# A fused attention and gated long convolution: turning the softmax weights of three batches by DMA instead of by TensorE, and cutting the last inverse transform by positions

## The chip, the core and the metric

The kernel runs on one core of a Trainium2 chip. A core has TensorE (PE, the matrix products; the loading of a product's stationary operand is shown apart as PEld), VectorE (DVE), ScalarE (ACT) and GpSimd (POOL). A further engine, SP, issues transfers, and so do POOL and ACT. The metric is the device time of one execution in microseconds (us), the median of several runs. A profile is one execution recorded by the hardware profiler. Its span runs from the first to the last instruction.

## What is computed

There are two chained attentions and then a gated convolution:

```
p_packed = softmax(scale * p @ k^T) @ v          # 32 packed queries per head
x        = softmax(scale * q @ p_packed^T) @ p_packed   # 576 positions, 8 heads of 64
proj     = x @ w_proj                            # 512 -> 3*512
x1, x2, x3 = proj split in three
x2_conv  = irfft(rfft(x2) * rfft(filter), n=576) # along the positions
out      = (x1 * x2_conv * x3) @ w_out
```

There are 8 batches. q, k and v have 8 heads, 576 positions and 64 features. The model width is 512.

## The kernel before

**The stages.** Each batch passes through four generator functions. `front` (lines 706 to 870) turns k and q, forms the first attention, and leaves the second attention's softmax weights: `a2`, 128 positions in the partitions by 4 tiles x 256 columns (8 heads x 32 packed keys), and a fifth tile of 128 columns with the last 64 positions, both halves of the keys side by side. The weights are normalised by one POOL product over 1152 columns (`a2n<-e,zr`, line 843; on DVE for batch 0). `turn` (872 to 932) multiplies the packed values into w_proj (`qm`, 892), takes the forward transform of the weights by products with constant tables (`fp`, `fpt`, 899 to 919; `ez` on ACT, then `fa` on POOL) and **turns the weights** so that the packed keys lie in the partitions: ten TensorE transposes of 128 columns per batch (`a2tp`, 923 to 929), five into each of two PSUM tiles, and one DVE copy of 576 columns per tile into `a2t` (930). `middle` (934 to 986) forms the spectrum (`f`, five pieces of 128 frequencies, 943), multiplies it by the filter on DVE (`tt`, 953) and combines it on POOL: two sums of 1024 columns (957) and four `gm` pieces of 512 (962); the fifth piece of `gm` comes from DVE. Beside it, `gate` (964) forms x1 and x3 as products of `qm` with `a2t`, 512 columns of positions at a time for each of four blocks of features, and a rest of 64. Per block x1 goes through an ACT copy (`x1s`) and a DVE product into `w`. `back` (989 to 1069) forms the inverse transform (`inverse`, 1018: `x2`, three products over the 288 even positions with `gm` 0, 1, 4 and three over the 224 odd ones with `gm` 2, 3, 4 per block of features), multiplies by `w` on DVE (`y`, 1030) and projects by w_out (`project_out`, 1033: `o`, five groups of positions, split in two halves of 256 columns in the last batch), from where ACT or DVE scale into `os` (5 buffers) and a transfer writes the result.

**The order.** All instructions are recorded first (`Recorder`, 221). `PRIORITY` (86) is a compressed list with one number for each instruction. It shifts the instruction's place in the recorded order. `plan` (306) gives these to `schedule` (316), which walks through the instructions with an estimate of each one's duration (`Op.ns`, 166; transfers in `transfer_ns`, 193) and takes, on each engine, the ready one with the lowest number. The order that comes out is then fixed for each engine (`emit`, 534). So the whole order, on all engines, hangs on the list: there is no loop order that survives it. All profiled instructions carry line 538, the line that emits them; they are told apart by the names of their tiles. In PE's gaps up to 34 us by the planner's clock, `spin` products (1112) that compute nothing are put in.

**Queues.** POOL issues all loads, which cast fp32 to fp16. SP issues the result's writes and, for batches 4 to 7, transposing DMAs: q turned into `qT` (one per batch, 16 blocks of 128x128), and for batches 6 and 7 the keys into `kT` (four per batch, 6 blocks of 96 rows each). SP works in order: a transfer that waits holds up those behind it.

Of the kernel before, what the change touches and what calls it, by code (L numbers as in the profile page):

```python
# [14 lines left out]
FP16 = mybir.dt.float16  # L15
AF = mybir.ActivationFunctionType
ALU = mybir.AluOpType
AX = mybir.AxisListType

P = 128  # L20
# [23 lines left out]
def _constants(S):  # L44
# [42 lines left out]
    'c-oy-2|QHm`#)ziBV@}q$-b}ILqe1#S<_+(QCblyS-Q3q6)7nx*OIa&WG5L#Qp%bw`;vWM;+D?&kC{0$!@d8{?{|OiG0r*f`<(aLzR&l0g<vs='  # L87
    '-skz=M^>B>C98^O79=;F+~z2#*^_&Aw(_gw@3h6d`$6M;p%eO@bfY=Fi=#RWN-2G@iNBm%a|9kab)~&68y;M>&-z&J>u@98+tu6WNM5tTp1|z#'
    'qN=p|rB#7u465h(xW9?n6X6(xO9%Y5o!Y~Vd5uTyvI9)Kk{_km+>Y2kq&E`(wW?P9sFRkdd!Sr^NE}AYes9%X?nBnbHmZ_nD-Bnas&><q?Gdd@'
    'agRzO9Fs4eI)1LutKQ+6yGz~G@Al~}em{~bQltED8=tkdw>WMUq+8?k^4OId=CA0)CUW!yJMK1h$A^2>XrHn<=si!HtR58dY7^%lTfApvBP(j}'  # L90
    'XK1H#MvGZi2Wh<=RN*mR3Ti#4ZRBGnWvrmze8J~}flqdhj1?a@tLLPO-KJTUX{YU%gA*f#YdP}n^tMYCwvDSg>leK~BH%1@WQaM_M%9T=PUB?X'
    'ZNCl=5AztGcz<EZH~dD8o>?L)TmO8V=kd$l)U2K-cHqeS4zwuGiM{S%C~vW(*VE9)(9JM5h3cXi-|Ml8<t)%=&!Q&>r6rE$u|9?z?(KcA{=p~2'
    'WY1y1W@QGqS;LH%|A&_L@z9f27oDSnnVpXDT~s#H_ElnbK5OM;d_j%<x*Ux?!yaX<l%j~Xw~?UKG`lX1oVp>~sxnV%xfQ#R=d%9MR9i00`{vFF'
    'lpvS1%pvy|ZPIRs9tYU%E!=j4u@Y;8jj!GJu-D}JPFv1=FRlrbmRaA218rDgjc`9%u+l2~1WPLK$-}SA1w4=V3tmv86_XyGw_n=6IwG#lHl)uc'
    'HO;MFtrvo808<2A_z&q%Vqe}^Rw@r>URiBD9C5CdcUW~-{554`eJ_*#DD!Wjz0m?~P{|CtUsvI-r(*UdahGo&4e2_;&BnBNStAatUoCUDoaE3?'
    'YDO<-)ckh*8vlDx;+)sPKm2ACs>QxzSOSHXxii&(FNRY!$)I%sdM*oVj`m265bg3{%S!G!@6~T$F&A6!`nvC3t1{1=k{?s2q7jFq>c0K9tzSFp'
    'a;AMHx?Kzfop-tJwDdLdm*6?6z$L^jZ+1d=hnb)0aeXzc-Whj)b_ruMN!`<W7p#wK$;nr0sVi}SUh!|EP7K;^MPHRQ)DFTLS=_xDqNv6(+cMsp'
    '08}ybEYk|{*$Bxn6ktS8@6%c3?3&`brYGg#>=k-2Le6%}t<<Q74-RVKAJ00)+WILgSEhSq+J}0FCwWAL-8*&5x@!L0W5(mUhwlV4J`r)2ZVa!%'
    ';(A1~2Esn+XDKJkq8TDJm_&*muvzU~)Irr4<Vx2HCXJSX#h+suRHkbF<P3X1UO!Z(Q{G*Rdb(6m)1KF{qNNq3e@5T$_ioeQbK4GYI$3Z6Ug>1#'
    '%#Ij$Po1h;3ZyxLxhf$b#QyA7<;`7RO}&e6mseJQoG3D#%zeh8a(*wLoVv=2x-h?~+X+2-Md|HIEYb?9iu^pg#94LpC2V%esbZJ4nYH$a@`~)_'  # L100
    '4tw*`o9zf+#Oe5nkHbr%g+_73+vsc?<TMSO1NVI5f5OTr|4~)>y<Z2%F?7EDDyPIN!(YsaQOceM=&`d(Sdm|hBJ7fX<<QP;OMLFtv7lq_cyCEi'
    'R-)ohVGHe7{g*}TI&{bH4@Eodr=fRYm6(s8$eL_lO2;|&UhH-0I-VEsywW2}HT=}djDkl9t*th{i2QGPld6Ly^qjRu(_@b^uEl6BajQ!4H<as%'
    'E{MjqT1>cz38x64#<VTpK7E~#_eXl!8&!<YL}TKZY<CJawAH6f%$dPp(SkQ)I;ME;fJ<Q1)pT6Z$mJEObA8`3%jZvo_}_oqnp*tjTxMCv$|Hdg'
    'lS0o^F6k~ISTie~u3(v+d`zmn<z;gXEkECmRgZnCrb+5-eewO<yBEE6_3yHq^P5sfvOab7eEwP)*I6=FTer~mSMj}6QF#H)@f$x*`FeC1F4b=x'
    '>M(ED3jd?kp3YuNyx&qx!tTKS)fP_I=IwKD_KRAp+IZQR7#JzA#JMd_?o4NmMTJUfObbYHpJ1z2qZguuB6}HSIRy(w>hr#>pa#Y)ZC>Y>%eU+f'
    '9Gr>#)HiU;Oih+;cu(;sZ@X)W?;@U`PCs4{Q~j=6RBH5?13w!Zzp`OGZ+Z9Ng$mD7W1L5@Wq`YvSFnX+LF=qM!>=7Y+a|Bw;+O9hKJb#QVrS%R'
    'acUde*N7KIv1Xp{s`wv#iOlR3K!>PADHaU<tm|D^$R0o|&^|WGIGh}meKl8;WzeZP>R{O2=Ald7I@aY41%ti8QggLU35?ssN8)^~3!Z?`ZadaX'
    'X`d4PT3%c`jnm3%sX+5=UKJ`k>t?Le!oM(ab5U40kA>aCh5ulua5c_7@wQuRwEMl={+Ay(2Ho-Uwfo~j?7cUJcWtjbI%_&#*74cD$NzAc+wFU1'
    ';l{yN4NymD`_-77r$4W*4%s}4?B5rK^LKb(9crN+_;V^>^U7Jrm^v=ruM4w`heV=^)7k@sVghpG-&)KZ{B$rbIk^G8LPM{|I|7)y(eB?X<6h-#'
    'ZrZs;*Tz%c!qX#8mgVf{=(wYA<i9)Azm6BIj=p<K_<2HR8msu7i?lL&30~*gbn;VC=iGnH+VDM9YoM<<G$@&~t4#fAcy_?U8@K&e>1Usf>QDaE'  # L110
    'Qi*is!<cS6irsb0H_SZ#v4H7Jt;Oc>olEDxT{E<f-aWEoyvg<uss}wh^j4eRO-tE0=sOGjwYxV1!Xg4M#iupp&9_%_wQm~ChZ2~al48=oEj{d*'
    '4y?`U&dI<fgyKHr)r8>^s*?um3!BsDlY+X_@4mV9BsJ~X%gBz37hzB7jGbB-yzb&UKBmW|NQ5}szdzX>)RWy*FW6V}>GgtT;_8)WuQDzs%XDmi'
    ')&05j`ZDv(Hfc^x-ATjCZi1{^VsTe;Ubg*ta)^aXceCawn^Ov#Xq#Ko3!I+cxffgA^}^ymsAI)hCYYA`mZy7P756q^goa}y+yZZS1EK;l82Gh<'
    'Z|$$CG`WMS1{3#cidB7YWO^TE9uE`XY1`)%rg3q<$`zM@ikO@OU2b{V+;aW%!;4GIM+=L&gsYT3WBb_4?p(~ayr)s<d9@^PuF3%YxZK}GJmV<N'
    'w~X%afV8BQtomSurLC@oDLwZgldp6sbQQgqJxv*lR5f>vt{T;adFNg@!`wH_q}af`{V!%7GzV>{#jlh58M||72U*$C$|ZFbzgG&|8k<&{D$8+`'
    '#nr_FjkW#tDY&A+?)1j&k@5Vh{+jZ^sZTZ4RrO=N<;NA3V|KjoJ#l1e_c<JcH*S(;{`u+Pcpv|$Or3z+$rtVC-X@mD#CR|D50B5I{KhALeV=X9'
    '>-+I#q^Zwt{#Pf9NrCAOqs-VJu5X^Y#pHWrVB32ZAXkT^QpRjX2p8`ck@7g~No-1OaLaJZCDvQt#p$s-w(2c$-i2ce%S$@y25iJPVU=WVHGdvs'
    'US2urNShJeUz?Xwno)~;RGRtnQFLN;Q)vKu2@}RxoxU+xzbMip!#Gwa-0G!i#+S;>&n4xr^P@OYq_N=|yw(9(jePO<6K1g-Y+M2#@}sqqf~O+j'
    '(|=uFO*#+3Qo98?=<>><C&lP~bVq1_JY8RNJ}vg$E3Mh~F;+E+_qzH02fl_qyb8IF#uYg;35F}Dw_n@e*;Q)idWQYS=yxV<UM0&9T(QXm%3@m-'
    'RciH5UvhQ*smqxhHTw2!RaFK19aix;&bce|FC|1d->Y$5WC)-a=Qb?hPnGA8i9|hYzu)_4aiS|jpy{gbN@`k>U{PiXlcv%@nYelGSpLVy2bd>W'  # L120
    'Wps8hXM`l)EctdPKmWJ&yrizAPD|?3telW+AA4W@F1Cd0X=dJA1!<p4lz!w<y|OZ^waIb2gzN*Ay>$tVEy_avNBj0PWU~D_%k`%Fyt4-1F`L{x'
    '$*yswxm79Fy6TddvW2l1_m_pci>7cKDxxL&N*G2a9$a`>Uq7h)w7+Oc<Q+RN-*oS?n5@DCYAcO0!{$byZspqyN|+mtp(`0a79Y|ZUd@hLnr^RW'
    '{7h5&p3RqOv8`nZJ^AAcCZ7(2+3e8SIC`jWVi|w|7=;4xfA|68e;|kgQ7909BfQZ7AYmQ`2^ap3pMXiCYd69(2oPTZ@-8rG5Y}Osynx&Y3#7-j'
    'ZDB+Rkpch|@<7^{C;<P<LDWvQKUo7vRF3y}ZICn&rI1MwZv^q8d`c1}O09hZ0@UuoWC!pXA;bt$$kwJHV!#L!_>aN0T|k(q4u(;rcu|%K14T3+'
    'c?H*Y0jUP?Uk$Ql1pVZIfK*`xVNw|2HCxu)C71&unI`N3!5}fR01{ysL=nsf)*QsU4Xt?&0pu?L5J@{Z&SZE%q=ofKgEp8=3JCr`MAQL6L^b3c'
    'Ng@a|0W>A~00u*i2co9{8G^L5)WG`vF9*>A3<g6>9cx00kX%v)n{cPaP$sBAO~L~KZZO#wa*{ww(C}75gt2a47$ye_fJv%B(gX2Jh+L7B?8C$`'
    '!o;KkWLd;m5F{akIzbx{^&bF7KoL1ZFcJ_DVG*L?Bvg^1MqO7(nkiI42Irbrz#0HyB-_9$wEiNO2u#TY3A}{=5Jas4zXDNMib7=|Ou!rxC87XC'
    '9W$6jYg7Y8PAy^kO=t?00e>T^|4e2`Fp>J(geLj`!W4c*Ds%0H293sR#M}LwXgfeAB_y7R9W=z9NYq4@p;^<g(F_nqNErmEfI$Hsl0Z^`A+l1U'
    'G`NBC$=pMIt%E;`T0M%2RjHzge?n2U7QBTtG*n#&2L9y$i3I@?3yly>8l;X8d=kI|A+FHS5HymrNp2M|Qp1Q5C>lao@S6h&nQp|vTBlj-%Orq-'
    '8yNwn>WUld4hakdfdG+?DS-cn+NCH4VCY{CczvTI%mHM6#{WR1%J3RdD2U<&saQd3Y$II;M8T8@!w9PJCleH*<Vd;^>&XdPg9bp^4llnEyC{JA'  # L130
    'Sb%Ud@mgaE=%4BiqMS_#{STsAfv6HkPBe&^4Ezs+N-K=8_y5ZdAo%z4{6}FzoJl={dKQ0}AiDx>@R|~NsvNKLcVp+K*Z@+zq4d9X)~(|~gp4S-'
    'qLdZ5?#w`uCc~LfSQJPC8yOR(YK;K!Psd1L-Ek2hn+a{~Jft0=zZpYTgFul~8k7~n;f1h5=IFl}LUl~0q>{p=z`EuIuS*UU@c@*Q*?NxrKThot'
    '$p'
# [3 lines left out]
class Op:  # L137
# [55 lines left out]
    def transfer_ns(self):  # L193

        far = self.ins[0] if self.reads == [] else self.out
        piece, size = far.shape[-1] * mybir.dt.size(far.dtype), far.size() * mybir.dt.size(far.dtype)
        self.piece_ns = max(piece / 25.2, 16) if piece > 1000 or self.engine == "POOL" else max(piece / 21.5, 17)
        if self.reads and self.engine != "POOL" and piece > 1000:
            self.piece_ns = piece / 22.7
        if self.what == "dma_start_transpose":  # L200
            piece, size, self.piece_ns = 256, self.out.size() * 2, 20
        return size / piece * self.piece_ns / 16
# [342 lines left out]
def kernel(  # L545
# [157 lines left out]
    APART = (0,)  # L703
    st = {}

    def front(b):
# [163 lines left out]
        s["a2n"], s["a2c"], s["R"] = a2n, a2c, R  # L870

    def turn(b):

        s = st[b]
        a2n, a2c, R = s["a2n"], s["a2c"], s["R"]
        qm = s["qm"] = sb([P, 2, DM3], FP16, tag="qm", name=f"qm_b{b}")
# [19 lines left out]
        a2t = s["a2t"] = sb([P, 2, S], FP16, tag="a2t", name=f"a2t_b{b}")  # L896
# [26 lines left out]
        for t in range(2):  # L923
# [10 lines left out]
    def middle(b):  # L934

        s = st[b]
        a2t, qm, fa = s["a2t"], s["qm"], s["fa"]
# [26 lines left out]
        def gate(*ms):  # L964
# [5 lines left out]
            for x, c0 in ((x1, 0), (x3, 2 * DM)):  # L970
                for m in ms:
                    for t in range(2):
                        nc.tensor.matmul(x[:, m - ms[0], :], qm[:, t, ds(c0 + m * P, P)], a2t[:, t, cols],
                                         start=(t == 0), stop=(t == 1))
# [14 lines left out]
    def back(b):  # L989
# [28 lines left out]
        def inverse(*ms):  # L1018

            cols = slice(0, MAIN) if len(ms) == 1 else slice(MAIN, S)  # L1020
            n = cols.stop - cols.start
            x2 = psm(f"x2_b{b}", [P, len(ms), n])
            for m in ms:
                todo = list(terms(x2[:, m - ms[0], :], m, cols))
                for i, (to, lhs, rhs) in enumerate(todo):
                    first = i == 0 if b in APART or len(ms) > 1 else i in (0, 3)
                    last = i == len(todo) - 1 if b in APART or len(ms) > 1 else i in (2, 5)
# [34 lines left out]
        for m in range(ND):  # L1062
            inverse(m)
            yield 660
# [87 lines left out]
```

## Time and profile before

| | |
|---|---|
| runs before | 189.7, 189.91, 190.37 us; median 189.91 us |
| the profiled execution's own time | 189.39 us |
| its span, first to last instruction | 187.6 us (1.8 us lie around it) |
| TensorE clock granted, mean | 0.994 |
| PE busy | 23.05 us of the first 30; 49.50 of the next 50; 69.99 of the next 70; 32.60 of the 32.6 up to 182.6 us |
| SP issues | 24 writes of 256 KB, 15 of 128 KB, 15 of 64 KB, 12 transposing DMAs |

A busy PE is not PE at its peak: the duration of one product contains the way through the array, and products overlap. What a product costs in a dense stream is the distance from one start to the next. In the chain of waits, a list in order of time, this is a row's length divided by its count. An in-order engine stalls where an instruction at its head waits for another engine, and everything behind waits with it.

### The profile page before, as it was taken

How to read it: one execution, taken by the hardware profiler on the slowest of the kernel's cores; microseconds unless marked ns; L12 is line 12 of the kernel's file. 1: busy time of each engine (PE TensorE's matmuls, PEld its weight loads, DVE VectorE, ACT ScalarE, POOL GpSimd, SP SyncE). 2: the span in 40 equal slices, each digit the busy share in tenths (PEclk: the TensorE clock that was granted, in tenths of full speed). 3: DMA queues.
4: the chain of work that ended last, by engine and by line, in shares of the span. 5: the costliest groups of instructions: out<-in, count | busy, mean ns of one | idle time of the engine just before them, and what ended most of it. 6: DMA issues, size and time to landing. Idle time of an engine off the chain costs nothing.

```text
span 187.6 us, 5689 instructions
## 1 busy us (share of the span) xinstructions
PE 175.1 (93%) x2363; PEld 112.5 (60%) x2363; DVE 145.3 (77%) x274; ACT 122.2 (65%) x261; POOL 138.0 (74%) x111
## 2 busy tenths in 40 slices
PE   0999879999999999999999999999999999999990
PEld 0456546666756766865577557657655566555770
DVE  7368797967569789977789978977688898796560
ACT  2457757758989988667965496469659934434240
POOL 7533447795966899989949997799189979979300
PEclk9999999999999999999999999999999999999997
DMA  5999999999999999999999999958601500332374
GB/s 145 297 200 196 204 204 201 259 203 188 200 227 275 177 202 192 148 131 188 263 197 225 158 156 200 179 133 272 166 2 59 169 3 0 121 103 59 121 256 131
DMA packets 49002, 31.96 MB, mean 170 GB/s; under 512 B 21008, under 2 KB 43920, under 8 KB 48976
## 3 DMA queue, kind: packets, MB, share of 16 engines
q0 software_dynamic: 29456, 17.11, 64.4%
q1 hardware_dynamic: 18944, 13.70, 31.7%
q10 hardware_dynamic: 576, 0.79, 1.6%
q8 instruction: 18, 0.29, 0.7%
q14 instruction: 8, 0.07, 0.1%
HBM read 35.39 MB, written 9.44 MB: 239 GB/s over the span
## 4 chain that ended last, share of the span: by engine, by line
PE 82%; DVE 7%; POOL 4%; ACT 3%; issue 1%; POOLq 0%; DVEq 0%
PE x_b L538 29%; PE o_b L538 17%; PE f_b L538 9%; PE fp_b L538 5%; PE s_b L538 4%; PE hp L538 4%; PE pv_b L538 3%; PE kTp_b L538 3%; PE qp_b L538 2%; PE a2tp_b L538 2%; DVE zs L538 2%; PE spin L538 1%; DVE tt L538 1%; POOL tt L538 1%; POOL a2n L538 1%; PE qTp_b L538 1%
## 5 line engine op out<-in xcount | busy, mean ns | idle before, releaser
L538 PE MATMUL x_b<-a2t,qm 128*128 128x64 f16 (+1 forms) x256 | 46.1, 286 | 0.8 <-ACT qm L538 0.7
L538 DVE TENSOR_TENSOR tt<-f_b,h 128x1024 f32<-128x1024 f32 x32 | 38.6, 1219 | 5.6 <-PE f_b L538 5.2
L538 POOL TENSOR_TENSOR gm<-tt,tt 128x512 f16<-128x512 f32 (+1 forms) x30 | 39.6, 1346 | 0.9 <-DVE tt L538 0.3
L538 POOL TENSOR_TENSOR tt<-tt,tt 128x1024 f32<-128x1024 f32 x14 | 33.2, 2378 | 8.5 <-DVE tt L538 8.4
L538 PE MATMUL o_b<-wout,y 128*128 128x512 f16 (+1 forms) x144 | 38.2, 356 | 0.0
L538 PE MATMUL x_b<-ac,gm 128*128 128x64 f16 (+3 forms) x300 | 36.6, 249 | 0.0
L538 ACT COPY x1s<-x_b 128x512 f32<-128x512 f32 (+1 forms) x40 | 21.8, 545 | 16.4 <-PE x_b L538 10.8
L538 DVE TENSOR_TENSOR w<-x1s,x_b 128x512 f32<-128x512 f32 (+1 forms) x40 | 24.7, 628 | 7.1 <-ACT x1s L538 4.5
L538 PEld LDWEIGHTS <-gm 128*128 128x128 f16 x300 | 23.1, 98 | 10.0 <-issue 1.0
L538 ACT ACTIVATE os<-o_b 128x512 f32<-128x512 f32 (+1 forms) x36 | 20.0, 572 | 11.2 <-PE o_b L538 10.8
L538 ACT CAST qm<-qp_b 128x512 f16<-128x512 f32 x48 | 25.4, 605 | 2.6 <-PE qp_b L538 2.5
L538 ACT ACTIVATE e<-s_b 96x384 f16<-96x384 f32 (+1 forms) x48 | 23.5, 524 | 4.2 <-PE s_b L538 3.7
L538 PE MATMUL f_b<-qm,fa 128*128 128x512 f16 x80 | 25.3, 379 | 0.3 <-POOL fa L538 0.3
L538 DVE SCALAR_TENSOR_TENSOR y<-w,x_b 128x512 f16<-128x512 f32 x32 | 21.2, 682 | 5.3 <-PE x_b L538 5.0
L538 PEld LDWEIGHTS <-qm 128*128 128x128 f16 x256 | 17.9, 98 | 11.3 <-ACT qm L538 1.2
L538 PEld LDWEIGHTS <-a2n 128*128 128x128 f16 x240 | 16.6, 98 | 9.1 <-DVE a2n L538 1.6
L538 POOL TENSOR_TENSOR fa<-ez 128x512 f16<-128x512 f32 x15 | 19.0, 1275 | 2.7 <-ACT ez L538 2.6
L538 POOL TENSOR_TENSOR a2n<-e,zr 128x1152 f16<-128x1152 f16 x7 | 14.9, 2130 | 4.5 <-DVE zr L538 4.4
L538 PEld LDWEIGHTS <-y 128*128 128x128 f16 x144 | 13.0, 98 | 7.4 <-issue 0.8
L538 ACT COPY ez<-fp_b 128x512 f32<-128x512 f32 x16 | 9.3, 591 | 5.7 <-PE fp_b L538 4.6
L538 DVE TENSOR_REDUCE zs<-e 128x36 f32<-128x1152 f16 (+2 forms) x10 | 11.1, 1107 | 0.9 <-ACT e L538 0.8
L538 POOL DMA_DIRECT2D kn<-in_k_dram x8 | 6.5, 815 | 6.8 <-PE s_b L538 2.4
(82 smaller groups left out, 288.5 us busy)
## 6 DMA issues: line engine op xcount, KB each, us to landing
out_dram<-os SPq DMA_DIRECT2D x24, 256.0 KB, 2.4
kn<-in_k_dram POOLq DMA_DIRECT2D x8, 576.0 KB, 14.9
vn<-in_v_dram POOLq DMA_DIRECT2D x8, 576.0 KB, 11.1
qn<-in_q_dram POOLq DMA_DIRECT2D x8, 512.0 KB, 14.2
out_dram<-os SPq DMA_DIRECT2D x15, 128.0 KB, 3.2
wp<-in_moe_w_proj_dram POOLq DMA_DIRECT2D x3, 512.0 KB, 15.9
w<-in_moe_filter_fft_dram SPq DMA_DIRECT2D x2, 512.0 KB, 6.2
out_dram<-os SPq DMA_DIRECT2D x15, 64.0 KB, 2.1
```

The lines of the kernel that those rows point to most:

```text
L538: ins = op.call(*op.args, **op.kw).ins
```

## The change

Three things are changed.

1. `FLIP = (5, 6, 7)`: for these batches `turn` no longer uses TensorE and DVE for the turned weights. SP issues one transposing DMA of `a2`, nine blocks of 128x128, into `a2t`, now 9 x 128 columns wide. The blocks lie in another order than the columns of `ac` and `w`, so `gate` takes the 512 positions in four pieces of 256, 64, 64 and 128 columns (two blocks of `a2t` in one piece, then halves of blocks, then one block). This makes 16 products instead of 4 for each block of features (x1 and x3 together).
2. In the last batch `inverse` works on two blocks of features and 256 positions at a time instead of one block and 512 positions. The even/odd boundary at 288 now falls in the second half: three products of 256 columns there were 288, and three of 32 are added. The number of DVE products stays at four.
3. A new `PRIORITY`. Every instruction may stand elsewhere. The estimate of a write's time in `transfer_ns`, which only the planner reads, is larger (piece / 18 instead of piece / 22.7).

```
 PRIORITY = (
...
         if self.reads and self.engine != "POOL" and piece > 1000:
-            self.piece_ns = piece / 22.7
+            self.piece_ns = piece / 18
...
-    APART = (0,)
+    APART, FLIP = (0,), (5, 6, 7)
...
-        s["a2n"], s["a2c"], s["R"] = a2n, a2c, R
+        s["a2n"], s["a2c"], s["R"], s["a2"] = a2n, a2c, R, a2
...
+        s["a2t"] = sb([P, 9 * P], FP16, tag="a2t", name=f"a2t_b{b}")
+        if b in FLIP:
+            nc.sync.dma_start_transpose(s["a2t"].rearrange("p (x r) -> p x r", r=P), s["a2"][:])
...
-        a2t = s["a2t"] = sb([P, 2, S], FP16, tag="a2t", name=f"a2t_b{b}")
+        a2t = s["a2t"].rearrange("p (t c) -> p t c", t=2)
...
-        for t in range(2):
+        for t in range(0 if b in FLIP else 2):
             tp = pst(f"a2tp_b{b}", [P, S], FP16)
...
-        a2t, qm, fa = s["a2t"], s["qm"], s["fa"]
+        a2t, a2b = (s["a2t"].rearrange(f"p (t c) -> p t c", t=x) for x in (2, 9))
+        qm, fa = s["qm"], s["fa"]
+
+        def turned(t, cols):
+
+            if b not in FLIP:
+                return [(slice(0, cols.stop - cols.start), a2t[:, t, cols])]
+            if cols.start:
+                return [(slice(0, 64), a2b[:, 4 + t, 64:128])]
+            return [(slice(0, 256), a2b[:, 2 + t:7 + t:4, :]), (slice(256, 320), a2b[:, 8, ts(t, 64)]),
+                    (slice(320, 384), a2b[:, 4 + t, 0:64]), (slice(384, 512), a2b[:, t, :])]
...
-                    for t in range(2):
-                        nc.tensor.matmul(x[:, m - ms[0], :], qm[:, t, ds(c0 + m * P, P)], a2t[:, t, cols],
-                                         start=(t == 0), stop=(t == 1))
+                    for pieces in zip(turned(0, cols), turned(1, cols)):
+                        for t, (c, right) in enumerate(pieces):
+                            nc.tensor.matmul(x[:, m - ms[0], c], qm[:, t, ds(c0 + m * P, P)], right,
+                                             start=(t == 0), stop=(t == 1))
...
-        def inverse(*ms):
-
-            cols = slice(0, MAIN) if len(ms) == 1 else slice(MAIN, S)
+        def inverse(*ms, cols=None):
+
+            cols = cols or (slice(0, MAIN) if len(ms) == 1 else slice(MAIN, S))
+            single = cols.stop <= MAIN and b not in APART
...
-                    first = i == 0 if b in APART or len(ms) > 1 else i in (0, 3)
-                    last = i == len(todo) - 1 if b in APART or len(ms) > 1 else i in (2, 5)
+                    first = i in (0, 3) if single else i == 0
+                    last = i in (2, 5) if single else i == len(todo) - 1
...
         for m in range(ND):
-            inverse(m)
+            if b == B - 1:
+                inverse(m % 2 * 2, m % 2 * 2 + 1, cols=slice(m // 2 * 256, m // 2 * 256 + 256))
+            else:
+                inverse(m)
             yield 660
```

## The prediction

> **What bounds the kernel now.** I read the page first: busy shares, the slices, the chain's shares.
>
> ```profile
> span 187.6 us, 5689 instructions
> ...
> PE 175.1 (93%) x2363; PEld 112.5 (60%) x2363; DVE 145.3 (77%) x274; ACT 122.2 (65%) x261; POOL 138.0 (74%) x111
> ...
> PE   0999879999999999999999999999999999999990
> ...
> DMA  5999999999999999999999999958601500332374
> ...
> PE 82%; DVE 7%; POOL 4%; ACT 3%; issue 1%; POOLq 0%; DVEq 0%
> ```
>
> PE is full from the second slice to the last but one, and the chain that ended last runs through it for 82% of the span. The transfers fill the slices up to 122 us; from 136 us on they are at 0 to 5 tenths until the last 10 us. Next, PE's own waits:
>
> ```profile
> PE spin L538 <- DVE ppk L538: 4.8, 1, 4.8
> PE x_b L538 <- ACT qm L538: 0.7, 1, 0.7
> PE a2tp_b L538 <- DVE a2n L538: 0.7, 2, 0.4
> ```
>
> After the first product at 4.8 us hardly any wait is large. So the time is PE's work plus small losses, and I need the price of a product in a dense stream. It comes from the chain in order of time (start, length, what):
>
> ```profile
> 150.95 0.29 PE fpt_b L538 x10
> ...
> 152.94 0.33 PE fp_b L538 x3
> 153.27 0.86 PE x_b L538 x4
> 154.13 0.17 PE a2tp_b L538 x3
> 154.30 0.24 PE x_b L538 x2
> ...
> 175.60 0.48 PE x_b L538 x5
> ...
> 182.61 0.02 issue
> 182.64 0.38 ACT os L538
> ```
>
> Start to start: 28.5 ns at 64 columns (fpt), 109 at 256 (fp), 215.5 at 512 (the four x_b), 56 at 128 (a2tp), 122.5 at 288 (the two x_b) and 96 at 224 (the last x_b row). The "mean ns" of the groups, 193 for 64 columns and 379 for 512, contain the pipeline and would mislead.
>
> All products but the spins, in order, at these prices (those that fill a part of the array at a quarter or an eighth of a full one: 16 qp_b of 512 columns stand in the chain with 0.56 us) come to 161.5 us. They start at 4.8 and end at 182.6. So PE loses some 16 us in its stream: 9 up to 30 us, while batch 0 fills the pipeline, and 7 later, in changes between tiled and full products and short waits; after 150 us 0.1 us.
>
> **The change, part by part.**
>
> *Transposes removed.* 3 batches x 10 products x 56 ns = 1.68 us of PE, all on the path. Beside them go 6 DVE copies of 576 columns (450 ns each, 2.7 us) and 6 uses of a PSUM tile; DVE is busy 77% and is not the bound, so I count these at nothing.
>
> *Gates in pieces.* A 512-column product at 215.5 becomes 109 + 28.5 + 28.5 + 56 = 222 ns: 6.5 ns more, for 4 blocks of features x 2 (x1, x3) x 2 halves of the keys x 3 batches = 48 products: 0.31 us added. The row that bears on it is the dense one: 64-column products, each with its own weights, follow each other at 28.5 ns, so weight loads are hidden even there.
>
> [...]
>
> *Inverse by halves.* Per block of features: three products of 288 become three of 256 and three of 32. The trace has no 32-column row; it lies between nothing and the 28.5 of 64 columns, and I take 28. 12 x (109 + 28 - 122.5) = 0.17 us added (lower end -0.16). DVE has the same four products. What it may give: positions 0 to 255 need `gm` 0, 1 and 4 alone, so their `y` no longer waits for POOL's last two pieces. Before, the end hid that wait behind batch 6's projections: the last 30 us of PE have no gap. So the gain here is nothing; it only lets batch 6's projections move forward (in the new order they all precede batch 7's).
>
> Sum of PE work: -1.68 + 0.31 + 0.17 = **-1.2 us**. One spin is added (25 to 26), in a gap. The number of changes between tiled and full products is equal in both orders (42).
>
> *Transposing DMAs.* Three on SP, each 1152 rows of 256 bytes. The trace has the same operation on other tiles: after the loads have ended, `kT` (576 rows) lands 2.6 us after issue, beside the loads `qT` (2048 rows) takes 11.4:
>
> ```profile
> kT<-kn SPq DMA_TRANSPOSE x2, 2.6
> ...
> qT<-qn SPq DMA_TRANSPOSE x4, 11.4
> ```
>
> The packets of the last `kT` take 0.87 us; twice the rows take twice that, so 2.6 + 0.9 = 3.5 us for `a2t`, with 11.4 as the other end. I take 3.5, since all three come after the last load (in SP's order they stand behind the last `kT`, issued at 122.3 us in the trace). SP itself is held 1.2 us by a `kT` and 1.9 by a late `qT`; 1.5 here.
>
> Who waits? In the new order I count PE work from the point at which the weights are there to the first gate that reads them. Batch 5: weights by 95 us of PE work (its first `fp`), first gate at 113.3, of which the `kT` in front on SP take 9: some 5 us to spare after landing. Batch 6: by 114 and 122.7, 5 to spare. Batch 7 is the tight one. In the trace its weights come 11.0 us after batch 5's last spectrum product:
>
> ```profile
> 138.78 0.22 PE x_b L538
> 139.00 0.43 PE f_b L538 x2
> 139.43 0.65 PE o_b L538 x3
> ```
>
> and on POOL
>
> ```profile
> 140.89 2.39 POOL L538 TENSOR_TENSOR tt<-tt,tt 128x1024 f32<-128x1024 f32 x1 [0.47 <-DVE tt L538]
> 143.36 4.96 POOL L538 TENSOR_TENSOR gm<-tt,tt 128x512 f16<-128x512 f32 x4
> 148.28 2.12 POOL L538 TENSOR_TENSOR a2n<-e,zr 128x1152 f16<-128x1152 f16 x1
> ```
>
> (139.4 to 150.4). The new order keeps this POOL sequence. From that product's end it has 12.0 us of PE work to the first `fp` of batch 7 and 15.3 to its first gate. So `fp` has 1.0 us to spare, and the DMA has 15.3 - 11.0 = 4.3 us, 0.8 more than 3.5. Behind this DMA on SP stands the last write of batch 4; batch 5's first result comes 12 us of PE work later and four of the five `os` buffers are free, so nobody waits. Behind batch 6's stands a write of batch 3, equally covered; behind batch 5's stand batch 2's writes, some 1.5 us later than they would be.
>
> [...]
>
> *The new order.* What it does to the 16 us of losses, the rows cannot say. The bounds: a tenth of them either way, 1.6 us. The start has the same products in nearly the same sequence; its loads are reordered a little (p before k). I take nothing, the middle.
>
> *The end.* POOL's last piece comes 9.1 us after batch 7's last spectrum product (166.15 to 175.29 in the trace). The new order wants it 9.8 us of PE work after that product, and the two spectra before it stand closer, which costs DVE about 0.3: 0.4 to spare. After PE's last product an ACT copy and a write remain, 5.0 us from 182.6 to 187.6, the same instructions in both.
>
> **Sum.** The profiled execution: span 187.6 - 1.2 = 186.4, time 189.39 - 1.2 = 188.2 us. It lies 0.5 us under the median of the runs, 189.91; from the median the forecast is **188.7 us**.
>
> **Rivals.** *The gain is given back as waits* (0.20). For: the new order is timed to fractions of a microsecond in two places (1.0 us before `fp`, 0.4 before the last `gm`). If POOL's last chain stayed at its old time, PE would reach the last `gm` 0.6 us early and half the gain would be left; one more such place leaves nothing: 189.3 to 190.4, with 189.9 for all of it.
>
> *The transposing DMA of batch 7 comes late, and the kernel is slower* (0.11). Place: the first gate of batch 7, where everything behind waits on PE. Price: each microsecond of landing beyond 4.3 is one of the time. Break-even is at 4.3 + 1.2 = 5.5 us; at the 6.3 us that is the median of all eight `kT`, +0.8, so 190.7; at 11.4 it is +5.9, so 195.8. For: SP is in order, and the writes of batches 4 and 5 share the engines. Against: the emptier DMA slices from 136 us on.
>
> *The order has new stalls of its own* (0.11): a tenth of 16 us more, -1.2 + 1.6 = +0.4, 190.3; two tenths, 191.9. Against: PE's waits before are small everywhere but at the start, and that is kept.
>
> *The order loses less* (0.08): a tenth of the losses go, such as the 0.7 us wait for `qm`: -2.8, 187.1.
>
> **How the numbers follow.** The forecast, -0.6 to -2.0 us, has 0.50. Within 0.3% (0.57 us, about what a measurement of this kernel can tell from no change) is the first rival, 0.20. Slower by more: 0.11 + 0.11 = 0.22. Faster: 0.50 + 0.08 = 0.58. The range runs from 187.1 to 190.9; it leaves out most of a late DMA and of two tenths of new stalls, about 0.15 together.
>
> **What would show it.** PE's count falls by 30 transposes and rises by 156 short products; the PE work sums to 160.3 us. `kT`-like DMA rows for `a2t` show 3 to 4 us to landing. A wait of PE on DMA `a2t` shows the second rival, waits on POOL `gm` or `a2n` the first. Wrong would be: 64-column pieces spaced far over 28.5 ns, or PE's first 30 us with more than 7 us idle.

## The result and the profile after

| | runs | median us | ratio to before, 95% interval |
|---|---|---|---|
| before | 6 | 190.39 | |
| after | 6 | 190.00 | 0.9981 [0.9958, 1.0004] |
| after, a second time | 12 | 190.09 | 0.9981 [0.9965, 0.9997] |

The forecast was 188.7 us, 0.6% less than the median of 189.91 us that was known then. What came is 0.2% less, about what can't be told from no change. In each of the two rows after, one run was slower than all others (193.71 and 192.1 us); the ratios leave these two out. The profiled execution of the kernel after took 189.83 us. That of the kernel before (189.39 us) was an early one: the medians of that kernel's later runs are 190.2 to 190.5 us, so a comparison of the two profiles shows less gain than the ratios.

The page of the kernel after (span; busy us, share, instructions; 40 slices; shares of the chain that ended last):

```profile
span 188.1 us, 5941 instructions
...
PE 175.7 (93%) x2490; PEld 117.4 (62%) x2490; DVE 143.3 (76%) x268; ACT 122.9 (65%) x261; POOL 137.8 (73%) x111
...
PE   0999979999999999999999999999999999999990
...
DMA  5999999999999999999999999999753450053635
...
PE 72%; DVE 12%; POOL 6%; DMA 4%; ACT 1%; issue 1%; SPq 1%; DVEq 0%; POOLq 0%
```

PE is as full as before, and there are 127 products more (30 transposes go, 156 short ones and a spin come). What changed is the chain: PE carries 72% of it where it carried 82%, DVE 12% where it had 7%. PE is waiting for others more often. But PE's own waits do not say where (engine, tile, releaser: us, times, longest):

```profile
PE spin L538 <- DVE ppk L538: 4.6, 1, 4.6
PE a2tp_b L538 <- DVE a2n L538: 1.1, 2, 0.6
PE hp L538 <- ACT gm L538: 0.7, 2, 0.4
PE s2t_b L538 <- ACT ppk L538: 0.4, 1, 0.4
PE s2t_b L538 <- issue: 0.3, 1, 0.3
PE x_b L538 <- DVE w L538: 0.2, 1, 0.2
```

The first four fall into the first 31 us, and no `a2t` and no last `gm` is among them. The places that the first two rivals named are quiet.

So the sum has to be made product by product. I take the start of every product in the trace, subtract the dense price of all products before it (the prices of the prediction, spins at nothing), and get PE's delay. Its growth is what PE loses. A number for the start (the delay at 16.2 us of work, where batch 0's gates have just begun) and one for all stalls behind it:

| profiled execution | PE work up to the last product, us | delay at the first gate | stalls behind it | of these, at changes of the array's tiling |
|---|---|---|---|---|
| before | 161.3 | 13.7 | 7.3 | 6.0 |
| after | 160.1 | 14.6 | 8.6 | 5.5 |
| after, a second time | 160.1 | 14.3 | 8.3 | 5.5 |

**Work fell by 1.2 us, as forecast. Stalls behind the start rose by 1.0 to 1.3 us** (0.5 less at the changes of tiling, two of which now stand ahead of batch 0's gates; 1.5 to 1.8 more elsewhere), and the start took 0.6 to 0.9 more. Two executions of the kernel after differ by 0.3 us in the stalls; of the kernel before there is this one profile alone. After the last product 0.5 us are won back (5.4 to 4.9). First profile: -1.2 + 0.9 + 1.3 - 0.5 = +0.5, the difference of the spans.

The new stalls are short and scattered. Five of them, the first with its product, from the timeline of the kernel after (start, us, engine, what; in brackets the idle time before and its releaser):

```profile
39.04 0.59 PE L538 MATMUL x_b<-ac,gm 128*128 128x512 f16 x2 [0.18 <-DVE w L538]
39.04 0.10 PEld L538 LDWEIGHTS <-gm 128*128 128x128 f16 x1 [0.30 <-issue]
...
58.41 0.10 PEld L538 LDWEIGHTS <-fa 128*128 128x128 f16 x1 [0.18 <-issue]
...
70.87 0.11 PEld L538 LDWEIGHTS <-fa 128*128 128x128 f16 x2 [0.27 <-POOL fa L538]
...
106.40 0.19 PE L538 MATMUL s2t_b<-ppk,qTm 128*128 128x64 f16 x1 [0.33 <-issue]
...
117.10 0.21 PEld L538 LDWEIGHTS <-kT 128*128 128x128 f16 x5 [0.30 <-issue]
```

Most stand at the weight load, not at the product, and show 0.2 to 0.3 us of idle time there. The table of PE's waits, in which I had looked for them, can't show them: while the load waits, the product before is still counted as busy (a product of 512 columns counts 379 ns, and the next starts after 215.5), and most of what is left lies under the 0.15 us from which the table counts. A change of tiling has a price too: in these two traces, behind the start, the first tiled product starts 68 to 96 ns beyond the dense price of the full one before it, and the first full one 130 to 132 ns after the last `pv_b` and 308 to 320 after the last `qp_b` where it waits for nothing else. Beyond the dense spacing and this price, the kernel before has six of over 0.14 us behind the start, 1.4 us together; the kernel after has ten, 2.6 us (2.4 in its second profile), between 39 and 134 us. The rest of the growth lies in smaller ones.

The trace's semaphores (the counters by which one engine tells another that it is done) name what most of the ten wait for. **Eight start 41 to 47 ns after the signal of an instruction of another engine that the product itself waits for**: DVE's `w` (39.04 and 117.09 us), `y` (45.87) and `tt` (56.79), ACT's `qm` (58.41), POOL's `a2n` (60.74), `fa` (70.88) and `gm` (72.10). The second profile has the same eight behind the same instructions. None of the products behind `w`, `y` and `tt` reads these; by the names, what comes free there are PSUM tiles that DVE had still to read. A ninth (134.07) starts 0.14 us after DVE's `ppn`, for which PE's queue had waited. Only the one at 106.40 us has nothing of the kind.

The transposing DMAs, from the view of the tile `a2t`:

```profile
L538 SPq DMA_TRANSPOSE a2t<-a2n x3: 1306/1348/1379, 124.4 to 151.6; - x3
...
DMA to landing us min/median/max: 3.3/4.6/4.9
```

Batch 7's is the last one (151.61 us, behind POOL's `a2n`, which ends at 151.59); it lands 3.3 us later, and the first gate that reads it starts at 155.28: 0.4 us to spare.

### The profile page after: what moved, and what is told of

It is laid out like the page before. It is cut to its first block, busy times and chain, and to the rows that moved or that the text cites. A ratio compares the mean times of both kernels' runs of the same rounds, so it can differ in the third digit from the quotient of the medians.

```text
span 188.1 us, 5941 instructions
## 1 busy us (share of the span) xinstructions
PE 175.7 (93%) x2490; PEld 117.4 (62%) x2490; DVE 143.3 (76%) x268; ACT 122.9 (65%) x261; POOL 137.8 (73%) x111
## 4 chain that ended last, share of the span: by engine, by line
PE 72%; DVE 12%; POOL 6%; DMA 4%; ACT 1%; issue 1%; SPq 1%; DVEq 0%; POOLq 0%
PE x_b L538 26%; PE o_b L538 15%; PE f_b L538 7%; DMA w<-in_moe_filter_fft_dram 4%; PE s_b L538 4%; PE fp_b L538 4%; DVE tt L538 3%; PE hp L538 3%; PE kTp_b L538 3%; POOL tt L538 3%; PE pv_b L538 3%; PE qp_b L538 2%; DVE w L538 2%; DVE zs L538 2%; POOL gm L538 1%
## 5 line engine op out<-in xcount | busy, mean ns | idle before, releaser
L538 PE MATMUL x_b<-a2t,qm 128*128 128x64 f16 (+3 forms) x400 | 44.5, 243 | 0.1
L538 POOL TENSOR_TENSOR tt<-tt,tt 128x1024 f32<-128x1024 f32 x14 | 33.1, 2379 | 10.3 <-DVE tt L538 10.2
L538 PE MATMUL o_b<-wout,y 128*128 128x512 f16 (+1 forms) x144 | 35.2, 356 | 0.0
L538 PE MATMUL x_b<-ac,gm 128*128 128x224 f16 (+5 forms) x312 | 34.9, 246 | 0.3 <-DVE w L538 0.2
L538 ACT ACTIVATE os<-o_b 128x512 f32<-128x512 f32 (+1 forms) x36 | 20.5, 574 | 15.0 <-PE o_b L538 14.4
L538 PEld LDWEIGHTS <-qm 128*128 128x128 f16 x400 | 24.4, 98 | 9.2 <-issue 1.5
L538 PEld LDWEIGHTS <-gm 128*128 128x128 f16 x312 | 21.8, 98 | 7.0 <-issue 1.6
L538 PEld LDWEIGHTS <-a2n 128*128 128x128 f16 x210 | 13.9, 98 | 6.6 <-DVE a2n L538 2.0
## 6 DMA issues: line engine op xcount, KB each, us to landing
qn<-in_q_dram POOLq DMA_DIRECT2D x8, 512.0 KB, 15.1
```

Source lines behind the costliest of these rows:

```text
L538: ins = op.call(*op.args, **op.kw).ins
```

## The experiments

All were timed in five rounds against the kernel before. Where an edit is to the order, the kernel carries the order of all engines as an explicit list, taken from one of the two kernels and changed only where said. The table gives the profile's account as above; its columns are the evidence behind each reading.

| run | ratio, 95% interval | PE work | delay at first gate | stalls behind |
|---|---|---|---|---|
| no_turn | 0.9922 [0.9895, 0.9950] | 159.6 | 14.6 | 7.7 |
| flip_old | 0.9977 [0.9953, 1.0001] | 159.9 | 14.3 | 9.4 |
| flip_late | 0.9962 [0.9937, 0.9986] | 159.9 | 14.2 | 8.2 |
| flip_mid | 0.9969 [0.9947, 0.9991] | 159.9 | 14.7 | 8.9 |
| flip_67 | 0.9911 [0.9891, 0.9932] | 160.4 | 14.0 | 7.4 |
| flip_67_again | 0.9923 [0.9904, 0.9942] | 160.4 | 14.2 | 7.4 |
| order_alone | 1.0071 [1.0049, 1.0094] | 161.4 | 14.7 | 8.8 |
| start_pv | 0.9953 [0.9928, 0.9979] | 160.1 | 13.7 | 8.1 |
| filter_back | 1.0011 [0.9985, 1.0037] | 160.1 | 15.1 | 8.8 |
| start_back | 1.0231 [1.0209, 1.0253] | 160.1 | 14.4 | 13.9 |
| flip_end | 1.0001 [0.9977, 1.0025] | 160.1 | 14.7 | 9.1 |
| whole_end | 1.0041 [1.0023, 1.0059] | 159.9 | 14.3 | 10.1 |
| pieces_64 | 1.0345 [1.0302, 1.0388] | 162.7 | 14.7 | 11.7 |
| pieces_late | 1.0028 [1.0009, 1.0048] | 161.9 | 14.6 | 7.4 |

The theory: the parts are worth what their PE work says, and the new order takes it back. The rival: the parts themselves bring the waits (the DMAs, the short products).

### Is PE work worth its time? no_turn

```
-        for t in range(2):
+        for t in range(0 if b in (5, 6, 7) else 2):
             tp = pst(f"a2tp_b{b}", [P, S], FP16)
```

> Leaves work out: before, without the transposes and copies of batches 5 to 7 and without any DMA in their place (the gates read what an earlier batch left); everything else as before, gates in one piece. Theory (PE work counts one for one): 1.7 us less, ratio 0.991. Rival (POOL's and DVE's chains set the time from there on): 0.996 to 1.000, and then no way of turning could have gained.

This kernel leaves out the transposes and their copies for three batches, so its results are not those of the program. 0.9922 is -1.5 us net, of 1.68 taken out. PE work counts nearly one for one in the old order.

### The parts in the old order: flip_old, flip_late, flip_mid

The kernel before's order, the three DMAs and the gate pieces in place of the products, no halves. They differ in SP's order alone:

```
 flip_old:   qT(7)  a2t(5)  kT(7) x4  writes of batch 2  ...
 flip_late:  qT(7)  kT(7) x4  writes of batch 2  a2t(5)  ...  writes of batch 3  a2t(6)
 flip_mid:   qT(7)  kT(7) x4  a2t(5)  writes of batch 2  ...  writes of batch 3  a2t(6)
```

> The order of before, with the turned weights of batches 5 to 7 by DMA and their gates in four pieces, each put where the product it replaces stood; the inverse uncut, no other instruction moved. Theory (the freed 1.2 us of PE work is real, and the new order's own losses of some 2 us took it back): PE work falls by 1.68 - 0.31 = 1.4 us, losses as before: ratio to before 0.992 to 0.994. Rival (POOL's and DVE's chains, or the DMAs, give any freed PE time back, whatever the order): 0.998 to 1.002.

0.9977, span 188.3 us: the gain is gone here too. On SP, batch 5's DMA stands ahead of the four `kT` of batch 7 (start, us held):

```profile
112.81 6.14 SPq L304 DMA_TRANSPOSE qT<-qn  x1
119.05 2.27 SPq L304 DMA_TRANSPOSE a2t<-a2n  x1
121.42 6.13 SPq L304 DMA_TRANSPOSE kT<-kn  x4
```

In the kernel before the `kT` were issued from 117.4 us on. PE then stalls 0.7 us at batch 7's scores (128.1 us) and 0.7 at a `qp_b` (133.2 us) that waits for a result buffer whose write stands behind all this.

> As flip_old (order of before, turned weights of batches 5 to 7 by DMA, gates in pieces, no halves), but on SP the DMA of batch 5 stands behind the key DMAs of batch 7 and behind the writes of batch 2, that of batch 6 behind the writes of batch 3. Theory (flip_old lost its gain because its DMA for batch 5 stood ahead of the four key DMAs of batch 7 on SP, which came 4 us later, and PE waited for these keys): PE work 1.4 us less, no new wait, ratio 0.992 to 0.994. Rival (the three DMAs themselves, wherever they stand, slow the transfers that PE waits for): 0.996 to 1.000.

The theory missed again (0.992 to 0.994 expected, 0.9962 measured). The two waits go and PE waits for batch 5's DMA itself, at 131.9 us:

```profile
PE x_b L304 <- DMA a2t<-a2n: 0.6, 1, 0.6
```

> As flip_late (the kernel before's order, transposing DMAs for batches 5 to 7, gates in pieces, no halves), but on SP the DMA of batch 5 stands right behind the last kT of batch 7 and ahead of batch 2's writes. Theory (the new parts are worth what their PE work says, and what lost it is the order around them): PE work 160.1 us as in flip_late, its one wait for a2t of 0.6 to 0.75 us at 131 us goes, so 0.992 to 0.994 of the kernel before, 188.8 us, span near 186.3. Rival (PE's gain comes back as waits wherever an order was made for other durations): another wait of the same size takes the place of that one, 0.996, as flip_late. Third case: batch 2's writes, now later, hold os buffers and PE waits for ACT os as in flip_old, 0.9975.

The theory missed (0.992 to 0.994 expected, 0.9969 measured) and the third case held: the wait for `a2t` went, and one for a result buffer came. ACT, and behind it PE, in flip_mid:

```profile
132.46 1.57 ACT L304 ACTIVATE os<-o_b 128x512 f32<-128x512 f32 x3 [0.67 <-DMA out_dram<-os]
...
133.11 1.38 PE L304 MATMUL qp_b<-wp,ppk 64*32 64x512 f16 x16 [0.66 <-ACT os L304]
```

Three places on SP gave three different sets of waits, 0.6 to 1.4 us of PE's time. SP takes these in turn (in flip_old the first `kT` starts 0.1 us after the 2.27 us of `a2t`), and it is full then: in the kernel before, from 104.3 to 128.1 us, two `qT` hold it for 12.9 us, four `kT` for 5.1 and six writes for 4.2. Batch 5's DMA, the writes and the last `kT` are all wanted just then.

### Without batch 5: flip_67

```
-    APART, FLIP = (0,), (5, 6, 7)
+    APART, FLIP = (0,), (6, 7)
```

on the kernel before's order, no halves, `a2t(6)` behind batch 3's writes.

> The kernel before's order, with the turning DMA and the gate pieces for batches 6 and 7 alone; batch 5 keeps its TensorE transposes; on SP batch 6's DMA stands behind batch 3's writes, as in flip_late. Theory (what the order of the kernel before can't take is batch 5's DMA, which meets the last kT and batch 2's writes on SP, whichever goes first): PE work -2 x 0.56 + 0.21 = -0.9 us, no wait of PE for a2t or os in the stretch from 119 to 136 us, stalls after the start 7.3 to 7.7 us as in the kernel before and no_turn, ratio 0.995 to 0.996, span near 186.9. Rival (any of these DMAs makes PE wait): a wait of 0.5 us or more for a2t or os moves to batch 6 or 7, ratio 0.998 or more.

> flip_67 once more, beside order_alone. Theory (its gain is PE work saved, 0.9 us, with nothing given back): 0.991 to 0.996. Rival (the first look was a lucky start): 0.997 or more.

0.9911 and 0.9923, the fastest of all: **188.47 and 188.80 us against medians of 190.16 and 190.30**. Stalls behind the start are back at 7.4. The DMAs land in 4.3 to 4.5 us. PE's waits from 31 us on, in flip_67, are two, and the same two as in the kernel before:

```profile
PE f_b L304 <- POOL fa L304: 0.3, 1, 0.3
PE fp_b L304 <- POOL a2n L304: 0.2, 1, 0.2
```

The medians gain 1.5 to 1.7 us where PE work fell by 0.9; by the profiles the rest would be the end behind the last product (0.6 less), but of the medians' surplus over the 0.995 to 0.996 expected I can't show the cause.

### The order without the parts: order_alone

The kernel after's order and halves, but all batches turned by TensorE and gates of 512 columns:

```
-    APART, FLIP = (0,), (5, 6, 7)
+    APART, FLIP = (0,), ()
```

> The new order without the turning DMAs and the gate pieces: the kernel after's order on all engines, but batches 5 to 7 are turned by TensorE and DVE again (the ten transposes of a batch in one row behind an earlier instruction of the order, each copy behind them) and the gates are products of 512 columns; the inverse by halves stays. PE work as the kernel before plus the halves' 0.17 us. Theory (the new order itself, not the DMAs or the pieces, costs 1.0 to 1.3 us of stalls after the start and 0 to 0.4 us in it): stalls after the start 8.2 to 8.7 us, ratio 1.006 to 1.009. Rival (the stalls belong to the DMAs and the short pieces, the order is as good as the old one): 7.3 to 7.7 us, ratio 1.001 to 1.002. The ten transposes in a row may add a wait for a copy of up to 0.5 us, which would show as a wait of PE on DVE a2t.

1.0071, in the theory's range: 1.35 us more than before, of which 0.17 is work. And nine of the ten stalls, from 39 to 117 us, stand at the same instructions as in the kernel after, of the same length to 0.06 us, the eight named above behind the same instructions of DVE, ACT and POOL. Four of them, from its timeline:

```profile
58.49 0.10 PEld L304 LDWEIGHTS <-fa 128*128 128x128 f16 x1 [0.18 <-issue]
...
70.95 0.12 PEld L304 LDWEIGHTS <-fa 128*128 128x128 f16 x2 [0.27 <-POOL fa L304]
...
106.42 0.19 PE L304 MATMUL s2t_b<-ppk,qTm 128*128 128x64 f16 x1 [0.28 <-issue]
...
117.12 0.21 PEld L304 LDWEIGHTS <-kT 128*128 128x128 f16 x5 [0.30 <-issue]
```

There is no turning DMA of the weights and no gate in pieces in this kernel, and the halves begin only after the last of these stalls. **The order carries the stalls.** The ten transposes of a batch in one row, which the new order did not have, brought no wait for a copy; among and behind them stand two stalls of 0.17 us (138 and 145 us), behind ACT's `ez` and `x1s`. The bookkeeping closes: order and halves +1.35, transposes and pieces -1.68 + 0.31 = -1.37 us, together nothing; measured -0.2% [-0.4, 0.0].

### The start: start_pv, filter_back, start_back, after_again

The kernel after, with one stretch at its beginning in the kernel before's order:

```
 start_pv:     up to batch 0's first product with v
 filter_back:  up to batch 0's first key transpose
 start_back:   up to batch 0's first gate, loads included
```

> The changed kernel with everything up to batch 0's first product with v in the order of before (filter first on SP, filter products and key transposes of batch 0 interleaved as before, k before p on POOL), the later loads as in the new order. Theory (the new order's loss in the start is the filter's late half, which holds the filter products and with them the keys of batch 0): first gate of batch 0 at 28.3 to 28.9 us instead of 29.4 to 29.6, ratio 0.993 to 0.996. Rival (the start's gain is lost again before the end): 0.997 to 0.999.

> The changed kernel with only the instructions up to batch 0's first key transpose in the order of before: both halves of the filter first on SP, ACT and DVE and PE accordingly, k before p on POOL. Theory (the third place of the filter's second half is the whole loss of the start): as start_back within 0.3 us, 0.992 to 0.995. Rival (the loss lies in batch 0's chain behind the filter): as after, 0.997 to 0.999.

> The changed kernel with all instructions up to the first gate of batch 0 in the order of before, loads included, and the rest in the new order. Theory (0.9 to 1.3 us of the new losses arise in the start, where the second half of the filter is issued third on SP): PE's first gate about 0.9 us earlier than after, ratio to before 0.992 to 0.994. Rival (the start is regained later, because POOL's chains set the end): as after, 0.997 to 0.999.

> The changed kernel unaltered, on the chip of the others. Theory: the filter's second half lands at about 10.5 us again, after some 2 us more than the first half of its own; PE's losses beside its work 2 us over before; ratio 0.996 to 1.000. Rival (the losses were one execution's chance): the second half lands near 8.5 us and the ratio is 0.993.

Not all loads are POOL's: those of the filter are issued by SP. after_again agrees with its first case: the filter's second half lands at 10.2 us (10.5 in the first profile, 8.6 in the kernel before), and the ratio is 0.9981. start_pv gives 0.9953; its delay at the first gate is the 13.7 of the kernel before, and its stalls behind the start are the kernel after's (8.1). That looks like a start worth 0.3%, but it is not shown: the intervals of start_pv and of the kernel after overlap, and whole_end (below), which begins with the same order on every engine, has a delay of 14.3, the kernel after's in its second profile. In filter_back neither case held (1.0011): the filter is there earlier, but its 34 products now stand ahead of the key transposes, and the delay is 15.1. start_back mixed two orders of the loads and lost 5.6 us behind the first gate, waiting for loads (`qn`, 14% of its chain); it says nothing on the question. The same instructions also differ from run to run at the start: 14.6 and 14.3 for the kernel after, 13.7 to 14.7 for the kernels that begin as the kernel before. So how much of the 0.6 to 0.9 us lost in the first profiles belongs to the order stays open; it may be nothing.

### The halves: flip_end, whole_end

```
 flip_end:   flip_mid's order up to batch 7's first inverse product, then the kernel after's, with halves
 whole_end:  start_pv's order up to there, then the kernel before's, inverse not cut
```

> flip_mid's order up to the first product of batch 7's inverse transform, from there the kernel after's order and its inverse by halves of positions (the rest of batch 6's projection ahead of it). Theory (the halves earn nothing, since the wait for the last gm was hidden already, and cost 0.17 us of PE work): 0.1 to 0.3 us slower than flip_mid, ratio 0.001 higher. Rival (the halves are what the new kernel earns at its end, where the kernel before has 0.5 us more from PE's last product to the end): 0.3 to 0.6 us faster than flip_mid, 0.990 to 0.992. Third: the last gm piece comes late for an order that was timed to 0.4 us, 0.3 to 0.6 us slower, with a wait of PE behind ACT or POOL gm after 165 us.

> start_pv's order (the new order with the start of the kernel before) up to batch 7's first inverse product, then the kernel before's order with the inverse not cut by halves. Theory (halves cost 0.17 us of PE work and bring 0.2 us of stalls between 150 and 170 us of PE work, as flip_end showed the other way round): 0.2 to 0.4 us less than start_pv, ratio 0.993 to 0.995. Rival (under the new order the halves do their work, the last gm piece would come late without them): a wait of PE for gm of 0.4 us or more in the last 20 us, ratio 0.996 to 0.998.

flip_end is 0.3% slower than flip_mid, with intervals that overlap; its profile shows the 0.17 us of work and one stall of 0.28 before `o_b`. The halves earn nothing in the old order. In whole_end neither case held as written: it is slower, 1.0041, but PE waits for DVE and not for `gm`. From its timeline (PE):

```profile
175.74 2.99 PE L305 MATMUL x_b<-ac,gm 128*128 128x288 f16 x31
179.95 0.28 PE L305 MATMUL o_b<-wout,y 128*128 128x256 f16 x1 [1.23 <-DVE y L305]
```

31 inverse products in a row, then the projection waits 1.23 us for `y`. In the kernel before, batch 6's projection stands between them and covers `y`. The new order has moved that forward, and the halves take over the cover. So they belong to the new order's end: neutral with it, and missing without it.

### The price of short products: pieces_64, pieces_late

In the kernel before, the gates' 512 columns in eight products of 64, for batches 1 to 7 (shown), and for 5 to 7:

```
-                    for t in range(2):
-                        nc.tensor.matmul(x[:, m - ms[0], :], qm[:, t, ds(c0 + m * P, P)], a2t[:, t, cols],
-                                         start=(t == 0), stop=(t == 1))
+                    cuts = [slice(c, c + 64) for c in range(0, n, 64)] if b and len(ms) == 1 else [slice(0, n)]
+                    for c in cuts:
+                        for t in range(2):
+                            nc.tensor.matmul(x[:, m - ms[0], c], qm[:, t, ds(c0 + m * P, P)],
+                                             a2t[:, t, cols.start + c.start:cols.start + c.stop], start=(t == 0), stop=(t == 1))
```

> Before with the 512-column gate products of batches 1 to 7 cut into eight of 64 columns each: 112 products become 896. Theory (64-column products with weights of their own stand 28.5 ns apart): 8 x 28.5 - 215.5 = 12.5 ns each, 1.4 us in all, ratio 1.007. Rival (weight loads bind in such a stream, at 56 ns or more each): 26 us and more, ratio 1.13 and up.

> The kernel before, with the gates' 512-column products cut into eight of 64 columns in batches 5 to 7 alone (48 products become 384), which PE reaches after 128 us, when the loads have ended. Theory (in pieces_64 the 4 us of stalls marked issue came from blocks of the instruction queue that arrived late because the loads filled the DMA): only the price of the products, 48 x (8 x 29 - 215.5) = 0.8 us, so 1.004 at most, and no stall marked issue above 0.2 us. Rival (short products run out of instructions wherever they stand): 48/112 of the 4 us come on top, 1.7 us, so 1.013, with stalls marked issue behind packets of the instruction queue after 128 us.

The spacing is 29 ns in both (the mean in pieces_64 is 29.3): the price I took holds. But pieces_64 lost 4.4 us more in stalls, which neither case foresaw, most of it in three places. From its waits, its timeline and its queues:

```profile
PE qp_b L306 <- issue: 1.4, 2, 1.2
PE a2tp_b L306 <- issue: 1.4, 1, 1.4
...
68.80 0.23 PE L306 MATMUL a2tp_b<-wc,a2n 128*128 128x128 f16 x1 [1.43 <-issue]
...
q8 instruction: 24, 0.39, 0.8%
```

PE waits there for nothing that the profile shows. The instruction queue moves packets of 16 KB, 24 in this kernel against 18 before; PE has 6316 instructions (weight loads counted) against 4748, so six packets more go with 1568 instructions more, by estimate some 261 in each. Three of the packets land at 67.4, 73.4 and 126.1 us, and PE's three long stalls end at 68.80, 74.72 and 127.40: 1.3 to 1.4 us after each. A block of instructions that isn't there in time would be such a stall. And counted through the trace, the three stalled products are PE's instructions 1986, 2242 and 4290: the second stands 256 behind the first, the third 2048, 8 times as many, behind the second. pieces_late has the same density of short products where the loads have ended, and no such stall (7.4): 1.0028, or 0.5 us, which the 0.6 us of added work explains. So the short products came with 4.4 us of stalls in pieces_64, where most of them run beside the loads, and with 0.1 in pieces_late, behind the loads. That the late block is the cause is inferred from these times and places; no run changed the blocks alone.

## Why the prediction failed, step by step

- **Transposes removed, -1.68 us of work: right.** no_turn gives -1.5 us. (That PE work fell by the 1.2 us forecast confirms the counts alone, since it is summed at the forecast's own prices; the prices are confirmed by the spacings in the next point.)
- **Gates in pieces, +0.31 us: right.** 256, 64 and 128 columns stand 109, 29 and 56 ns apart in the kernel after.
- **Inverse by halves, +0.17 us and no gain of its own: right** (the products of 32 columns stand 27.5 ns apart, 28 were taken), and incomplete. That the projections of batch 6 move forward was named; that the halves are then what covers `y` (1.23 us without them) was not.
- **Transposing DMAs: the mechanism right, the size too small.** 3.3 to 4.9 us to landing for 3.5. Batch 7's slack was counted as 4.3 us and is 3.7; nobody waits.
- **The new order: "What it does to the 16 us of losses, the rows cannot say ... I take nothing, the middle."** This is the step that failed. It costs 1.0 to 1.3 us behind the start, which is the gain, and 0 to 0.9 in it; order_alone puts order and halves together at 1.35. The mechanism is the third rival's, "the order has new stalls of its own", with 1.2 us in place of 1.6, but I gave it 0.11. The first rival has the time right and the places wrong: not the first `fp` or last `gm` of batch 7, but ten stalls of 0.14 to 0.5 us between 39 and 134 us, nine of them waits for DVE, ACT and POOL.
- **"PE's waits before are small everywhere but at the start, and that is kept"**: the argument against that rival read the wrong table. PE's waits leave out those of its weight loads and all under 0.15 us; from 31 us on that table has 0.5 us in the kernel before, of 7.3 us of stalls.
- What I had not weighed: in the old order the change would have failed as well, as long as batch 5 was in it. SP has no room at 119 to 128 us (in flip_mid three `kT`, batch 5's DMA and two writes hold it for 8.2 of the 8.3 us from 120.28 us on). I had checked that the DMA's landing was in time, and for what stood behind it on SP only the writes, in the new order.

What stays open: the stall at 106.40 us. It fits late instructions. It is 0.50 us in one execution and 0.18 in a second; at the same place of the same order it is 0.44 in order_alone, 0.73 in whole_end, and absent in start_pv and filter_back. Where it stands it ends 1.4 to 1.6 us after an instruction packet has landed, and its product is PE's instruction 3009 (3010 in whole_end), 1023 (1024, 4 times 256) behind the first of pieces_64's three, which stand 256 and 8 times 256 apart. No run tried it. No run moved one of the other stalls' instructions either, so what the order could gain by that is not known.

## What to carry to other kernels

Work taken off the bounding engine is worth its time only in an order that stays dense; a new searched order is a part of the change with a price of its own, here as large as the gain, and it can be measured alone, by running it without the parts. Before giving an in-order queue one more transfer, list everything that it issues in those 10 us and who waits for each: three places for one DMA gave three different waits, and with that one batch left out the gain came, 1.5 to 1.7 us. Sum stalls from the starts of products, weight loads included, and not from the table of waits; then ask of each which instruction it was waiting for.

## What the hardware showed

- In pieces_64 PE's weight loads sat idle for 1.66, 0.58 and 1.46 us at three places where the profile shows no releaser, each until 1.3 to 1.4 us after a 16 KB packet of the instruction queue had landed. In pieces_late, where the short products stand behind the loads, they cost their 29 ns and no such stall.
- A transposing DMA of 1152 rows held SP for 1.3 to 2.6 us and landed 3.2 to 4.9 us after its issue (the kernel after, flip_old, flip_late, flip_mid, flip_67, flip_end and whole_end); those of q (2048 rows) held SP for 1.9 to 7.9 us in the kernel before.
- In both profiles of the kernel after, the eight stalls that wait for an instruction of DVE, ACT or POOL end 41 to 47 ns after that instruction's signal.
- With the same first instructions, the delay at the first gate differs by up to 1.0 us between executions (13.7 in the kernel before, 14.7 in flip_mid), nearly as much as the whole change was to bring.
